# A fused attention and MLP kernel: its instruction order planned anew, with another rule for GpSimd and VectorE at their shared port

## The chip, the cores and the metric

The kernel runs on one core of one Trainium2 chip. What counts is the device time of one execution, in microseconds. Three runs of the kernel before took 1088.69, 1086.15 and 1087.42 us, a median of 1087.42 us. One more execution was profiled; all rows below are from that one.

## What is computed

A linear attention over 8 batches, 8 heads, 576 positions and 64 dimensions, with 128 features and their exponentials of both signs, and behind it an MLP over the 4608 tokens, from 512 to 2048 and back, with the exact GELU:

```python
proj = einsum('bhsd,df->bhsf', x, w_phi)            # x is q, then k
proj = proj - max(abs(proj), axis=-1)
phi = concatenate([exp(proj), exp(-proj)], axis=-1)
kv, z = einsum('bhsf,bhsd->bhfd', k_p, v), k_p.sum(axis=2)
attn = einsum('bhsf,bhfd->bhsd', q_p, kv) / (einsum('bhsf,bhf->bhs', q_p, z) + 1e-6)
x = attn, heads side by side, 4608 x 512
h = x @ w_in                                        # 512 x 2048
out = gelu(h) @ w_out                               # 2048 x 512
```

Both weights arrive as 64-bit floats. The MLP is multiplied in parts: each operand is split into a rounded high part and a low part, and three of the four products are summed.

## The kernel before

**Attention, batch by batch.** For keys, TensorE projects a quarter of a batch's heads into `pk`, VectorE takes the largest absolute value of each row (`mx`, L439) and subtracts it (`ek`, L375), both reading PSUM; ScalarE takes the exponentials, and TensorE sums `kv`. For queries the features lie on the partitions: TensorE makes `pq`, ScalarE copies it to `pc` in SBUF, GpSimd finds the largest of all partitions (`mb`, an all-reduce, L511), VectorE subtracts it, ScalarE takes the exponentials `ef`. From batch 2 on the denominators go another way: VectorE weights the exponentials (two operations of L553 and two of L556, `pc` again), GpSimd adds over the partitions (`db`, L522), and the sums travel through DRAM (`d_d`, `dc`, then `r_d` with the reciprocals of L621). `mb` and `db` have one buffer each.

**Weights.** In `split_weight` each of 32 pieces of 128x512 is turned from two 32-bit words into a float and split: a DMA, an Abs on ScalarE, two operations of VectorE with a scalar (L391, L393), two with a scalar and a tensor (L395, L397), a cast on ScalarE (the high half) and a subtraction on VectorE (L375, the low half). `w_i3_3` is the last piece of the first matrix, `w_o12` to `w_o15` the last four of the second.

**MLP, 18 blocks of 256 tokens.** For block j, `tokens` loads `xr` and the spread reciprocals `xh` (DMAs of L667 and L670), and VectorE makes the product `xr`, its rounded copy `xh` and the rest `xl`. Then eight steps u: 24 matmuls into `ph_j_u`, two GELUs on ScalarE (`gh`, and `ph` in place), the subtraction `gl` on VectorE, and for each of two pieces f the 6 matmuls of `po` that take `gh`, `gl` and `w_o`f. `ph` has two buffers, `po` one. Blocks 0 to 7 run beside the attention of later batches; blocks 8 to 17 use sums of weights (`ts`, L749, made on VectorE beside blocks 2 to 7) to save matmuls, and no attention stands beside them.

**What sets the order.** All operations go into a `Plan`. Its `order` simulates the five engines with a cost for each operation and picks, again and again, the operation that could start first (among those that could start at the same time on one engine, the one with the lowest rank). `emit` then writes the operations by their planned start, and each engine executes its own in that order. The planner has a rule for a port that GpSimd and VectorE share: while a GpSimd all-reduce reads (for `READS` us from its start, `port[1:]`), VectorE's operations with `port` set are not begun. The operations `mx`, `ek` and `gl`, which read PSUM, are exempt (`port=False`). Constants at the file's end set times, biases and slacks.

Of the kernel before, what the change touches and what calls it, by code (L numbers as in the profile page):

```python
# [62 lines left out]
class Plan:  # L63
# [8 lines left out]
    SHAPE = {"f": 0, "k": 1, "q": 1, "v": 2, "n": 2, "w": 3, "d": 4}  # L72
    READS = {"max": 1.12, "add": 2.38, "max main": 1.99, "add main": 4.23, "max rest": 1.0, "add rest": 2.12}
    SPENT = {"max": 2.28, "add": 3.8, "max main": 3.75, "add main": 6.45, "max rest": 2.07, "add rest": 3.42}
    WINDOW = 3.413
# [37 lines left out]
    def order(self, bias):  # L113
# [6 lines left out]
        clock = dict.fromkeys(engines, 0.0)  # L120
# [9 lines left out]
        port = [0.0, 0.0, 0.0]  # L130

        def start_of(o):
            t = max(clock[o.eng], o.ready)
            if o.eng == "pool" and o.port:
                t = max(t, port[0])
            if o.table == "exp" and table[0] == "gelu" and gelus[0] % (2 * STICK):
                t = max(t, left_at[0] + PATIENCE)
            seen = {}
            for b in o.bufs:
                if not b.held and b.tag is not None:  # L140
# [6 lines left out]
                    t = max(t, when)  # L147
                    seen[b.tag] = i + 1
            if o.eng == "dve" and o.port and port[1] <= t < port[2]:
                t = port[2]  # L150
# [21 lines left out]
        while len(done) < n:  # L172
            best = None
            for e, lst in cand.items():
# [3 lines left out]
                for o in lst:  # L178
                    t = start_of(o)
# [12 lines left out]
                key = None  # L192
                for t, o in opts:
                    if t <= lim:
# [5 lines left out]
                        if key is None or (k, o.n) < key[0]:  # L200
                            key = ((k, o.n), t, o)
                if best is None or key[1] < best[1]:
                    best = key
            if best is None:
                raise RuntimeError("no operation can go")
            _, t, o = best
            cand[o.eng].remove(o)
            cost = o.cost
# [3 lines left out]
            if o.eng == "pe":  # L212
                if self.SHAPE[last[0]] != self.SHAPE[o.kind]:
                    cost += self.BEHIND[last[0]] + self.BEFORE[o.kind]
                last[0] = o.kind
            o.start, o.end = t, run(t, cost, o.duty) if o.eng == "pe" else t + cost
            if o.nbytes:
# [3 lines left out]
            if o.table == "gelu":  # L221
                gelus[0] += 1
                left_at[0] = o.end
            clock[o.eng] = o.end + (0.45 if o.eng == "pool" else 0.0)
            if o.eng == "dve" and o.port:
                port[0] = o.end
            if o.eng == "pool" and o.port:
                port[1:] = [o.start, o.start + self.READS[o.port]]
            for b in o.bufs:
# [62 lines left out]
def fused_kernel(ctx: ExitStack, tc: tile.TileContext, qT, kT, va, w_st, w_in, w_out, out):  # L292
# [207 lines left out]
    def q_front(nm, n, load, kb, k, main):  # L500
# [9 lines left out]
        most = f"max{main}"  # L510
        op("pool", plan.SPENT[most], lambda: nc.gpsimd.partition_all_reduce(  # L511
            mb(), pc(), P, bass_isa.ReduceOp.absmax), r=[pc], w=[mb], port=most, **k(1))
# [350 lines left out]
SUMSAT = 177.8  # L863
SUMSEACH = 5.81
SUMSPAN = 311.59
T15 = 926.21
T18 = 982.3
BIAS = 89.44
STICK = 2
# [14 lines left out]
LEAD = 161.66  # L884
HOLD = 13.76
WR = -32.15
ATR = -58.86
AT = 194.75
POOLSLACK = 0.3
DMASLACK = 0.5  # L890
T0 = 91.27
# [43 lines left out]
```

## Time and profile before

| | before |
|---|---|
| median of 3 runs | 1087.42 us |
| the profiled execution, own time | 1086.7 us |
| its span, first to last instruction | 1084.9 us |
| TensorE busy | 1038.2 us (96%) |
| VectorE busy | 697.5 us (64%) |
| ScalarE busy | 616.5 us (57%) |
| GpSimd busy | 305.4 us (28%) |
| mean granted TensorE clock | 0.982 |

In the rows, PE is TensorE, DVE is VectorE, ACT is ScalarE, POOL is GpSimd and SP the engine that issues most DMAs. L12 is line 12 of the kernel. A name as `w_i` stands for all tiles with a number behind it. In a timeline the bracket at a row's end gives the engine's idle time just before it, and what ended it. The clock of a stretch is a share of full speed: 1.00 is 2.4 GHz, 0.50 is 1.2 GHz.

### The profile page before, as it was taken

To read this page: it belongs to the slowest core of one execution; us is meant where nothing else is said; L and a number is where in the kernel's file an instruction comes from. 1 tells how busy PE (TensorE), PEld (TensorE's weight loads), DVE (VectorE), ACT (ScalarE), POOL (GpSimd) and SP (SyncE) were. 2 spreads that over 40 slices of the span, in tenths; PEclk is the share of its full clock that TensorE was granted. 3 is DMA by queue.
4 is the path that set the end of the run, shared out by engine and by line. 5 is a ranking of instruction groups with operands and counts; after the bars stand their busy time and mean duration, and the time that the engine had idled before them with its cause. 6 is when DMAs were issued, how large, how long until landed. Compare 5 with 4: busy or idle time off the path is not lost.

```text
span 1084.9 us, 23613 instructions
## 1 busy us (share of the span) xinstructions
PE 1038.2 (96%) x9763; PEld 900.0 (83%) x9763; DVE 697.5 (64%) x1228; ACT 616.5 (57%) x1008; POOL 305.4 (28%) x77
## 2 busy tenths in 40 slices
PE   7979995999998999999999999999999999999997
PEld 5646664787786787777788879999999999999997
DVE  5999999688977788665344332555565565565554
ACT  4868785666666687667656653434344344344343
POOL 2232234346556453564654451000000000000000
PEclk7999998999999999999999999999999999999999
DMA  8486660344444335324212145620120120120000
GB/s 285 137 249 190 175 218 27 96 134 134 131 128 130 112 127 146 103 66 124 58 55 75 35 126 173 214 59 20 40 60 11 50 60 16 45 59 20 21 21 21
DMA packets 87180, 107.08 MB, mean 99 GB/s; under 512 B 29168, under 2 KB 56832, under 8 KB 87072
## 3 DMA queue, kind: packets, MB, share of 16 engines
q1 hardware_dynamic: 86928, 105.30, 31.9%
q8 instruction: 77, 1.26, 0.5%
q14 instruction: 31, 0.25, 0.1%
q10 hardware_dynamic: 144, 0.26, 0.1%
HBM read 75.87 MB, written 29.66 MB: 97 GB/s over the span
## 4 chain that ended last, share of the span: by engine, by line
PE 80%; DVE 8%; DMA 4%; ACT 3%; issue 3%; POOL 1%; SPq 0%; DVEq 0%; ACTq 0%; POOLq 0%
PE ph L334 33%; PE po L334 14%; PE pa L334 10%; PE pb L334 7%; PE kv L334 5%; PE pn L334 4%; PE pk L334 2%; PE pq L334 2%; DMA xh<-r_d 1%; DMA x_d<-xo 1%; DVE pc L375 1%; DVE pc L553 1%; DVE ts L375 1%; PE pn_rest L334 1%; POOL mb L511 1%
## 5 line engine op out<-in xcount | busy, mean ns | idle before, releaser
L334 PE MATMUL ph<-xh,w_i 128*128 128x256 f32 x2304 | 419.8, 279 | 7.0 <-DVE w_i L375 5.1
L334 PEld LDWEIGHTS ph<-xh,w_i 128*128 128x128 f32 x2304 | 359.4, 189 | 21.0 <-issue 12.2
L334 PE MATMUL ph<-xl,w_i 128*128 128x256 f32 x1152 | 320.1, 278 | 0.0
L334 PEld LDWEIGHTS ph<-xl,w_i 128*128 128x128 f32 x1152 | 217.9, 189 | 0.3
L522 POOL PARTITION_ALL_REDUCE db<-pc x24 | 151.0, 6290 | 137.2 <-DVE pc L556 112.7
L375 DVE TENSOR_TENSOR sg<-ga 128x256 f32<-128x256 f32 (+1 forms) x240 | 84.6, 376 | 153.2 <-ACT ga L780 151.4
L334 PE MATMUL po<-w_o,gh 128*128 128x512 f32 (+1 forms) x518 | 165.8, 402 | 5.0 <-DVE w_o L375 5.0
L511 POOL PARTITION_ALL_REDUCE mb<-pc x36 | 121.2, 3368 | 161.9 <-ACT pc L369 128.2
L780 ACT ACTIVATE ga<-ph 128x512 f32<-128x512 f32 x80 | 47.8, 598 | 168.7 <-PE ph L334 168.7
L334 PEld LDWEIGHTS po<-w_o,gh 128*128 128x128 f32 x518 | 94.5, 190 | 34.4 <-DVE w_o L375 5.3
L334 PE MATMUL pa<-w_o,oh 128*128 128x256 f32 x640 | 112.8, 276 | 0.0
L334 PE MATMUL po<-w_o,gl 128*128 128x512 f32 (+1 forms) x281 | 102.9, 381 | 7.1 <-DVE gl L375 7.1
L334 PEld LDWEIGHTS pa<-w_o,oh 128*128 128x128 f32 x640 | 96.3, 188 | 0.0
L334 PE MATMUL pa<-w_o,ol 128*128 128x256 f32 x320 | 88.3, 276 | 0.0
L375 DVE TENSOR_TENSOR gl<-ph,gh 128x512 fp32r<-128x512 f32 x64 | 43.7, 685 | 67.5 <-ACT ph L704 67.5
L334 PE MATMUL pn<-ef,kvn 128*64 128x512 f32 (+2 forms) x288 | 80.5, 561 | 5.6 <-ACT xo L369 5.6
L334 PE MATMUL pb<-tw,uh 128*128 128x256 f32 x480 | 85.6, 276 | 0.0
L516 ACT ACTIVATE ef<-pc 128x1024 f32<-128x1024 f32 (+1 forms) x72 | 68.1, 972 | 17.5 <-DVE pc L375 17.2
L444 ACT ACTIVATE ek<-ek 128x1024 f32<-128x1024 f32 x64 | 67.6, 1058 | 15.5 <-DVE ek L375 15.0
L334 PEld LDWEIGHTS pb<-tw,uh 128*128 128x128 f32 x480 | 72.2, 188 | 0.0
L334 PEld LDWEIGHTS po<-w_o,gl 128*128 128x128 f32 x281 | 53.9, 192 | 21.3 <-DVE gl L375 9.6
L703 ACT ACTIVATE gh<-ph 128x512 fp32r<-128x512 f32 x64 | 38.2, 597 | 54.2 <-PE ph L334 52.1
(84 smaller groups left out, 1620.8 us busy)
## 6 DMA issues: line engine op xcount, KB each, us to landing
vt<-in_va_dram SPq DMA_DIRECT2D x32, 325.0 KB
t_d<-ts SPq DMA_DIRECT2D x40, 256.0 KB
out_dram<-ob SPq DMA_DIRECT2D x35, 256.0 KB
kt<-in_kT_dram SPq DMA_DIRECT2D x32, 256.0 KB
raw_i<-in_w_in_dram SPq DMA_DIRECT2D x16, 512.0 KB
raw_o<-in_w_out_dram SPq DMA_DIRECT2D x16, 512.0 KB
qt<-in_qT_dram SPq DMA_DIRECT2D x28, 256.0 KB
x_d<-xo SPq DMA_DIRECT2D x24, 256.0 KB
```

Of the source, the lines that this page charges most:

```text
L334: return tc.keep_in_program_order(nc.tensor.matmul(*a, **kw))
L375: op(eng, cost, lambda: e.tensor_tensor(out=dst(), in0=a(), in1=b(), op=o), r=r, w=w, **kw)
L444: op("act", act(256 * n), lambda s=s: nc.scalar.activation(e[s](), e[1](), AF.Exp, scale=1.0 - 2.0 * s), r=[e[1]], w=[e[s]], table="exp", ...
L511: op("pool", plan.SPENT[most], lambda: nc.gpsimd.partition_all_reduce(mb(), pc(), P, bass_isa.ReduceOp.absmax), r=[pc], w=[mb], port=most, ...
L516: op("act", act(2 * n), lambda s=s: nc.scalar.activation(ef[s](), pc(), AF.Exp, scale=1.0 - 2.0 * s), r=[pc], w=[ef[s]], table="exp", **k())
L522: op("pool", plan.SPENT[total], lambda: nc.gpsimd.partition_all_reduce(db(), pc()[:, :2], P, bass_isa.ReduceOp.add), r=[pc], w=[db], port= ...
L553: op("dve", dve(n, fast=True) + 0.06, lambda pc=pc, ef=ef, one=one, j=j: nc.vector.tensor_scalar(out=pc()[:, j], in0=ef[0]()[:, j], scalar ...
L703: op("act", act(2 * TB, True) + 0.016, lambda gh=gh, ph=ph: nc.scalar.activation(gh(), ph(), AF.Gelu), r=[ph], w=[gh], table="gelu", rank= ...
L780: op("act", act(2 * TB, True) + 0.037, lambda ph=ph, ga=ga: nc.scalar.activation(ga(), ph(), AF.Gelu), r=[ph_all], w=[ga], table="gelu", a ...
```

## The change

No operation is added or taken out. The planner is told other things, and the order comes out anew.

- An all-reduce of GpSimd no longer waits in the plan for VectorE's current operation at the port: its place in the order is the time at which its operand is ready. Its work begins when VectorE's operation ends, and from then on VectorE's port operations are held for `READS`.
- Where a GpSimd operation could start at the same time as another engine's, it is put first.
- `READS` grows by 0.07 to 0.22 us an operation, `SPENT` (its whole length) falls by 0.13 to 0.34, and a gap of 0.45 behind each GpSimd operation goes.
- The constants `SUMSEACH` (pace of the weights' sums), `BIAS` (against switching ScalarE's table), `HOLD` (earliest start of batch 1) and `DMASLACK` change.

```diff
@@ Plan
-    READS = {"max": 1.12, "add": 2.38, "max main": 1.99, "add main": 4.23, "max rest": 1.0, "add rest": 2.12}
-    SPENT = {"max": 2.28, "add": 3.8, "max main": 3.75, "add main": 6.45, "max rest": 2.07, "add rest": 3.42}
+    READS = {"max": 1.2, "add": 2.45, "max main": 2.15, "add main": 4.45, "max rest": 1.1, "add rest": 2.2}
+    SPENT = {"max": 2.14, "add": 3.59, "max main": 3.54, "add main": 6.11, "max rest": 1.94, "add rest": 3.23}
@@ start_of
-            if o.eng == "pool" and o.port:
-                t = max(t, port[0])
@@ order
-                if best is None or key[1] < best[1]:
+                if best is None or key[1] < best[1] or key[1] == best[1] and e == "pool":
                     best = key
...
-            o.start, o.end = t, run(t, cost, o.duty) if o.eng == "pe" else t + cost
+            o.start = t
+            if o.eng == "pool" and o.port:
+                t = max(t, port[0])
+                port[1:] = [t, t + self.READS[o.port]]
+            o.end = run(t, cost, o.duty) if o.eng == "pe" else t + cost
...
-            clock[o.eng] = o.end + (0.45 if o.eng == "pool" else 0.0)
+            clock[o.eng] = o.end
...
-            if o.eng == "pool" and o.port:
-                port[1:] = [o.start, o.start + self.READS[o.port]]
@@ constants
-SUMSEACH = 5.81
+SUMSEACH = 5.49
-BIAS = 89.44
+BIAS = 103.27
-HOLD = 13.76
+HOLD = 16.53
-DMASLACK = 0.5
+DMASLACK = 0.3
```

The orders of both kernels hold the same instructions on TensorE, VectorE, GpSimd and SyncE; ScalarE has two loads of its function table fewer. Three places follow, all on VectorE.

**First place: ahead of the low half of `w_i3_3`**, for which the last matmuls of `ph_0_7` wait. The last operation (L556) of `pc_2_0_0` is the operand of the all-reduce `db_2_0_0`. Before:

```order
L556 SCALAR_TENSOR_TENSOR pc_2_0_0_1686<-ef_2_0_0_1_1834,kvn_2_0_0_1376,pc_2_0_0_1686 128x512
L395 SCALAR_TENSOR_TENSOR wt_i3_3_1928<-raw_i3_3_1709,wt_i3_3_1928 128x512
L391 TENSOR_SCALAR wt_o12_1946<-wt_o12_1946 128x512
L397 SCALAR_TENSOR_TENSOR wt_i3_3_1928<-raw_i3_3_1709,wt_i3_3_1928 128x512
L393 TENSOR_SCALAR wt_o12_1946<-wt_o12_1946 128x512
L553 TENSOR_SCALAR pc_2_1_0_1729<-ef_2_1_0_0_1843,kvn_2_0_1_1649 128x512
L395 SCALAR_TENSOR_TENSOR wt_o12_1946<-raw_o12_1774,wt_o12_1946 128x512
L375 TENSOR_TENSOR w_i3_3_1959<-wt_i3_3_1928,w_i3_3_1959 128x512
```

After:

```order
L556 SCALAR_TENSOR_TENSOR pc_2_0_0_1720<-ef_2_0_0_1_1855,kvn_2_0_0_1582,pc_2_0_0_1720 128x512
L397 SCALAR_TENSOR_TENSOR wt_i3_3_1838<-raw_i3_3_1658,wt_i3_3_1838 128x512
L391 TENSOR_SCALAR wt_o12_1885<-wt_o12_1885 128x512
L556 SCALAR_TENSOR_TENSOR pc_2_0_0_1720<-ef_2_0_0_1_1855,kvn_2_0_0_1582,pc_2_0_0_1720 128x512
L375 TENSOR_TENSOR w_i3_3_1937<-wt_i3_3_1838,w_i3_3_1937 128x512
L439 TENSOR_REDUCE mx_2_1_1_1948<-pk_2_1_1_1872 128x8
L375 TENSOR_TENSOR ek_2_1_1_1_1965<-pk_2_1_1_1872,mx_2_1_1_1948 128x1024
L393 TENSOR_SCALAR wt_o12_1885<-wt_o12_1885 128x512
L391 TENSOR_SCALAR wt_o13_1950<-wt_o13_1950 128x512
L395 SCALAR_TENSOR_TENSOR wt_o12_1885<-raw_o12_1717,wt_o12_1885 128x512
```

Five operations (three of `pc_2_1_0`, namely its subtraction and the two of L553, and two of `wt_o12`; some stand above the rows shown) are no longer ahead of `w_i3_3`'s subtraction, and this comes directly behind the operation on which `db_2_0_0` waits.

**Second place: ahead of `w_o15`**, which the matmuls of `po_0` for f = 15 take. The operand of the all-reduce `db_2_1_0` is `pc_2_1_0`; before, its last operation stands 12 rows ahead of the first row here, in front of `w_o13`. Before:

```order
L397 SCALAR_TENSOR_TENSOR wt_o14_1986<-raw_o14_1870,wt_o14_1986 128x512
L391 TENSOR_SCALAR wt_o15_2084<-wt_o15_2084 128x512
L393 TENSOR_SCALAR wt_o15_2084<-wt_o15_2084 128x512
L395 SCALAR_TENSOR_TENSOR wt_o15_2084<-raw_o15_1949,wt_o15_2084 128x512
L375 TENSOR_TENSOR w_o14_2100<-wt_o14_1986,w_o14_2100 128x512
L397 SCALAR_TENSOR_TENSOR wt_o15_2084<-raw_o15_1949,wt_o15_2084 128x512
L375 TENSOR_TENSOR gl_1_0_2145<-ph_1_0_2070,gh_1_0_2126 128x512
L375 TENSOR_TENSOR w_o15_2143<-wt_o15_2084,w_o15_2143 128x512
```

After:

```order
L395 SCALAR_TENSOR_TENSOR wt_o15_2140<-raw_o15_1933,wt_o15_2140 128x512
L375 TENSOR_TENSOR w_o14_2147<-wt_o14_2091,w_o14_2147 128x512
L397 SCALAR_TENSOR_TENSOR wt_o15_2140<-raw_o15_1933,wt_o15_2140 128x512
L556 SCALAR_TENSOR_TENSOR pc_2_1_0_1752<-ef_2_1_0_1_2094,kvn_2_0_1_1848,pc_2_1_0_1752 128x512
L375 TENSOR_TENSOR xr_2_1511<-xr_2_1511,xh_2_2020 128x1024
L375 TENSOR_TENSOR w_o15_2172<-wt_o15_2140,w_o15_2172 128x512
L556 SCALAR_TENSOR_TENSOR pc_2_1_0_1752<-ef_2_1_0_1_2094,kvn_2_0_1_1848,pc_2_1_0_1752 128x512
L371 CAST xh_2_2020<-xr_2_1511 128x1024
L375 TENSOR_TENSOR gl_1_0_2211<-ph_1_0_2030,gh_1_0_2184 128x512
L375 TENSOR_TENSOR er_3_1_2213<-pk_3_r_2013,mx_3_r_2083 128x512
L375 TENSOR_TENSOR gl_1_1_2233<-ph_1_1_2064,gh_1_1_2228 128x512
```

The last operation of `pc_2_1_0` now stands behind `w_o15`, and behind it come one rounding copy, then `gl_1_0`, `er_3_1` and `gl_1_1`, which read PSUM; `gl_1_0` has moved behind `w_o15`, and `xr_2` ahead of it.

**Third place: ahead of `gl_3_0`**, which the first `po` matmuls of block 3 take. Before:

```order
L556 SCALAR_TENSOR_TENSOR pc_4_0_0_3777<-ef_4_0_0_1_3883,kvn_4_0_0_3399,pc_4_0_0_3777 128x512
L375 TENSOR_TENSOR ts_4_4_3910<-ts_4_4_3910 128x256
L556 SCALAR_TENSOR_TENSOR pc_4_0_0_3777<-ef_4_0_0_1_3883,kvn_4_0_0_3399,pc_4_0_0_3777 128x512
L375 TENSOR_TENSOR pc_4_1_0_3832<-pc_4_1_0_3832,mb_4_1_0_3870 128x1024
L375 TENSOR_TENSOR xr_4_3001<-xr_4_3001,xh_4_3745 128x1024
L375 TENSOR_TENSOR gl_3_0_3957<-ph_3_0_3885,gh_3_0_3940 128x512
```

After:

```order
L375 TENSOR_TENSOR gl_2_7_3888<-ph_2_7_3688,gh_2_7_3861 128x512
L375 TENSOR_TENSOR ts_4_4_3826<-ts_4_4_3826 128x256
L375 TENSOR_TENSOR pc_4_0_0_3801<-pc_4_0_0_3801,mb_4_0_0_3842 128x1024
L375 TENSOR_TENSOR gl_3_0_3907<-ph_3_0_3846,gh_3_0_3890 128x512
L439 TENSOR_REDUCE mx_5_0_0_3931<-pk_5_0_0_3911 128x8
L375 TENSOR_TENSOR ts_5_0_3933<-w_o13_2081,w_o5_1154 128x512
L620 TENSOR_SCALAR dc_3_1_3885<-dc_3_1_3885 128x4
L375 TENSOR_TENSOR ek_5_0_0_1_3950<-pk_5_0_0_3911,mx_5_0_0_3931 128x1024
```

Before, `gl_3_0` comes behind `xr_4`, whose operand `xh_4` is loaded by DMAs; after, `xr_4` stands behind `gl_3_1`, and the two last operations of `pc_4_0_0`'s sum behind `gl_3_0` as well. On SyncE the last loads of `xh_4` now stand behind a store of `ts_4_4` and a load of `kt_5_0_1`.

Two more shifts are used below without a listing. On VectorE the `xl_0` of the first block is instruction 94 before and 103 after, with `w_o4`'s and `w_o5`'s first operations, `w_i3_1` and `pc_1_1_0` now ahead of it. On TensorE, all 24 matmuls of `ph_1_0` and 12 of `ph_1_1` now stand ahead of the `po_0` matmuls with `w_o12`, and the attention's `kv_2_1_1` and `pn_2_1_0` ahead of those with `w_o13`; before, `ph_1_0` came in halves behind `w_o12`'s and `w_o13`'s.

## Rows read from the trace of the kernel before

**Rows 1.** The page: busy time of TensorE, and its clock in 40 slices.
```profile
PE 1038.2 (96%) x9763; PEld 900.0 (83%) x9763; DVE 697.5 (64%) x1228; ACT 616.5 (57%) x1008; POOL 305.4 (28%) x77
...
PEclk7999998999999999999999999999999999999999
```

**Rows 2.** Busy time by stretch: stretch, length, each engine's busy time, granted clock, DMA.
```profile
60.00:100.00 40.00, 34.36 (x390) 22.79 (x387) 37.51 (x49) 30.94 (x49) 15.55 (x5) 0.96 0.75 202
...
160.00:200.00 40.00, 26.58 (x221) 23.37 (x220) 34.01 (x41) 19.31 (x28) 13.96 (x2) 0.83 0.17 55
200.00:340.00 140.00, 138.48 (x1472) 111.23 (x1471) 114.69 (x155) 96.76 (x146) 76.39 (x18) 1.00 0.43 133
...
360.00:660.00 300.00, 298.36 (x2795) 239.68 (x2794) 164.78 (x221) 199.91 (x269) 162.75 (x37) 1.00 0.32 93
660.00:1079.00 419.00, 419.00 (x3662) 417.51 (x3661) 225.27 (x585) 167.24 (x365) 0.00 (x0) 1.00 0.17 54
```

**Rows 3.** Timeline of TensorE, 158 to 363 us: start, length, operation, idle before.
```profile
163.33 0.39 PE L334 MATMUL ph<-xh,w_i 128*128 128x256 f32 x1 [1.97 <-ACT w_i L369]
...
168.89 0.79 PE L334 MATMUL ph<-xh,w_i 128*128 128x256 f32 x2 [5.06 <-DVE w_i L375]
...
176.43 0.71 PE L334 MATMUL pk_r<-wst,kr 64*128 64x128 f32 x8 [1.34 <-DVE ek L375]
...
188.10 0.79 PE L334 MATMUL po<-w_o,gh 128*128 128x512 f32 x1 [5.04 <-DVE w_o L375]
...
351.22 0.79 PE L334 MATMUL po<-w_o,gl 128*128 128x512 f32 x1 [4.38 <-DVE gl L375]
```

**Rows 4.** Busy time in three stretches of the lower clock (columns as rows 2).
```profile
165.60:172.30 6.70, 3.41 (x16) 3.41 (x17) 6.70 (x10) 1.91 (x3) 3.33 (x1) 0.50 0.00 0
...
186.10:192.80 6.70, 4.70 (x18) 4.31 (x18) 4.94 (x7) 0.62 (x1) 0.34 (x1) 0.50 0.00 0
349.90:356.60 6.70, 5.38 (x16) 4.51 (x17) 6.67 (x10) 2.34 (x2) 1.17 (x1) 0.50 0.11 40
```

**Rows 5.** Timeline of VectorE, 155 to 200 us.
```profile
158.67 0.48 DVE L553 TENSOR_SCALAR pc<-ef,kvn 128x512 f32<-128x512 f32 x1
...
162.88 4.76 DVE L553 TENSOR_SCALAR pc<-ef,kvn 128x512 f32<-128x512 f32 x1
...
168.16 0.68 DVE L375 TENSOR_TENSOR w_i<-wt_i,w_i 128x512 fp32r<-128x512 f32 x1
...
180.59 4.56 DVE L391 TENSOR_SCALAR wt_o<-wt_o 128x512 f32<-128x512 f32 x1
185.18 1.54 DVE L393 TENSOR_SCALAR wt_o<-wt_o 128x512 uint32<-128x512 uint32 x1
...
189.39 0.69 DVE L375 TENSOR_TENSOR w_o<-wt_o,w_o 128x512 fp32r<-128x512 f32 x1
```

**Rows 6.** Timeline of GpSimd: one mb and the three db of these places.
```profile
146.90 3.54 POOL L511 PARTITION_ALL_REDUCE mb<-pc  x1 [3.25 <-DVE pc L375]
...
161.17 7.76 POOL L522 PARTITION_ALL_REDUCE db<-pc  x1 [10.73 <-DVE pc L556]
180.24 6.20 POOL L522 PARTITION_ALL_REDUCE db<-pc  x1 [11.31 <-DMA d_d<-db]
...
344.05 7.02 POOL L522 PARTITION_ALL_REDUCE db<-pc  x1 [3.09 <-DVE pc L556]
```

**Rows 7.** Timeline of VectorE beside the mb at 146.90 us.
```profile
147.25 1.21 DVE L439 TENSOR_REDUCE mx<-pk 128x8 f32<-128x1024 f32 x1
148.50 1.23 DVE L375 TENSOR_TENSOR ek<-pk,mx 128x1024 f32<-128x1024 f32 x1
```

**Rows 8.** Timeline of VectorE, 338 to 361 us.
```profile
346.60 3.97 DVE L375 TENSOR_TENSOR xr<-xr,xh 128x1024 f32<-128x1024 f32 x1 [1.51 <-DMA xh<-r_d]
350.49 0.68 DVE L375 TENSOR_TENSOR gl<-ph,gh 128x512 fp32r<-128x512 f32 x1
```

**Rows 9.** Busy time from 330 to 410 us (columns as rows 2).
```profile
330.00:410.00 80.00, 75.62 (x786) 60.47 (x785) 63.46 (x84) 58.56 (x83) 41.44 (x9) 0.96 0.40 124
```

**Rows 10.** Timeline of TensorE, 60 to 100 us.
```profile
78.87 1.19 PE L334 MATMUL pn<-ef,kvn 128*65 128x288 f32 x4 [3.19 <-ACT xo L369]
```

## The prediction, made before the change was timed

> **What bounds the kernel now.** The page's totals come first: TensorE is busy 1038.2 us [rows 1] of a span of 1084.9, so all other engines together cost it 46.7 us. The clock's 40 slices show where: it is low at the start, in the slice from 163 on, and nowhere else by much [rows 1]. The table by stretch says it sharper. From 160 to 200 TensorE works 26.58 of 40 us at a clock of 0.83; from 200 to 340 it loses 1.5 us, from 360 to 660 1.6, and behind that nothing [rows 2]. So whatever TensorE loses before 360 us arrives at the end one for one, since nothing later has slack to give it back, and what stops it before 200 and at 350 is what an order can change. The timeline of TensorE names those stops: 1.97, 5.06, 1.34 and 5.04 us between 160 and 190, all for weights or for VectorE's `ek`, and 4.38 us at 351 for `gl` [rows 3]. Behind each long stop the clock stands at 0.50, that is 1.2 GHz, for a stretch [rows 4]: TensorE had stood idle just before, and pays for the stop twice.
>
> Why VectorE is late there is read from its own timeline. An operation with a scalar that takes 0.48 us at 158.67 takes 4.76 at 162.88, and two more take 4.56 and 1.54 at 180.59 and 185.18 [rows 5]. Beside them GpSimd's two `db` all-reduces run, from 161.17 and from 180.24 [rows 6]. Operations that read PSUM are not held: `mx` and `ek` keep 1.21 and 1.23 us beside the `mb` at 146.90 [rows 6, 7]. So a hold costs the path only if what stands behind it on VectorE is awaited by TensorE, and behind these two stand the low halves of `w_i3_3` and of `w_o15` [rows 5].
>
> **The change, part by part.** It moves work, adds none, and the sum is therefore made of stops that go and stops that come. It is made against the profiled execution, 1086.7 us, which lies 0.7 under the median of the runs shown.
>
> *First and second place.* The four stops there come to 1.97 + 5.06 + 1.34 + 5.04 = 13.4 us. In the two slow stretches TensorE does 3.41 and 4.70 us of work [rows 4], which at the full clock takes half: (3.41 + 4.70) / 2 = 4.1 us more. Together 17.5 us could go.
>
> How much does? `w_i3_3` is ready at 168.16 + 0.68 = 168.84. In the new order five operations are no longer ahead of it, 2 x 0.48 + 0.42 + 0.68 + 1.23 = 3.3 us (the 0.42 from operations of the same form in that timeline, the 0.68 and the 1.23 from [rows 5, 7]), and the hold, 4.76 - 0.48 = 4.3 us, falls behind it: 168.8 - 3.3 - 4.3 = 161.2, when TensorE has just got there. That stop goes, and the ScalarE half of it with it, since its operand comes earlier by the same operations. The hold does not vanish. It now meets `wt_o12`, first covered by `mx` and `ek` of batch 2 (2.4 us, reading PSUM), and it still delays `gl_0_6`, which stands four operations behind: I put it at 168.1. As `ph` has two buffers, `ph_1_0` waits for that: some 1.5 us of a stop remain. The second hold, 4.08 and some 1.1 us, fell ahead of `w_o15`; now its operand is ready only behind `w_o15`, one operation of 0.68 may still meet it, and then `gl_1_0`, `er_3_1` and `gl_1_1` pass. Counting VectorE's operations through, `w_o15` comes at 181.8 + 1.1 = 182.9 instead of 189.39 + 0.69 = 190.1; TensorE, not stopped before, wants it about 1.5 us earlier. On GpSimd nothing else is queued behind these two `db`s until 202 that a batch needs sooner.
>
> One thing speaks against this. `xl_0` now has nine more operations ahead, some 5.6 us at these durations, so the first MLP block may begin later by 0 to 5.6 us. VectorE is busy 37.51 of 40 us there [rows 2], so little of it is hidden by idleness; but attention operations that TensorE would have done in between now come earlier, and holds in the old order fall away. I take 2.0. First and second place: 17.5 - 1.5 - 1.5 - 2.0 = 12.5 us, between 9 (the whole 5.6 lost) and 15.
>
> *Third place.* `xr_4` is held until 350.57 and `gl_3_0` behind it until 351.2 [rows 8], while `db_4_0_0` runs [rows 6]. In the new order `gl_3_0` stands ahead of `xr_4` and of the operations on which that `db` waits. The 4.38 us go, and half of the 5.38 us of work in the slow stretch behind it [rows 4]: 4.4 + 2.7 = 7.1 us. What is late next is `xl_4`, wanted only by block 4, some 60 us on.
>
> *What comes.* TensorE's order has one change of kind more, which my count of its rows prices at 0.5 us (0 to 1). And an earlier TensorE asks for `gl` earlier: from 330 to 410 VectorE is busy 63.46 of 80 us with the stop in it [rows 9], and none of that work becomes less. I allow for one new stop of the size of the one at 351, 4.4 us (0 to 7.1, the whole of the third place). What it would be exactly, the trace of before can't show, as TensorE is late there already.
>
> Sum: -12.5 - 7.1 + 0.5 + 4.4 = -14.7, so 1086.7 - 14.7 = 1072.0 us.
>
> A rule to be weighed. The rows show a `db` that began at 161.17 and ended at 168.93, while the held operation had ended at 167.64, and VectorE's other operations ran for 1.7 us beside its start [rows 5, 6]. The Trainium skill, "SBUF — State Buffer", section "Who interferes with whom", says that whoever issues first gets the shared ports "for the whole instruction" and the other fully blocks. By that, a hold would last to the end of `db`, 1.3 us longer here, and `gl_0_6` would come 1.3 us later, so 1073.3. The row decides for the shorter hold at the first place; at the second the two slow operations together end at 186.72 where `db` ends at 186.44, so there the rule nearly fits.
>
> **The rivals.** *Only the first half comes.* If VectorE is what sets the pace from 330 to 410, the 7.1 us of the third place return as stops at later `gl`s. For it speaks that it is 79% busy there and that a `db` hold is 4.3 us each time; against it, that from 360 to 660 TensorE loses 1.6 us in 300. Time: 1086.7 - 12.5 + 0.5 + 4.4 = 1079.1, from 1077 to 1084 with the first places at their lower end and a second stop.
>
> *It doesn't do what it says.* GpSimd's operations begin at the same events as before; only a plan is different. If the holds fall on operations as urgent as before (on `gl_0_6` for a full 4.3, on a `w_o` for another), the first places keep only the 3.3 us of removed work less the 2.0 of a late start, and a stop like the third one comes back: about 1086, no change.
>
> *Slower.* The mechanism is the start: from 60 to 100 TensorE already waits 3.19 us for ScalarE's `xo` [rows 10], and VectorE is at 94%. In the new order `pk_1_1_0`, two weights and `xr_0` (whose `xh_0` comes by DMA) stand where VectorE must wait for another engine. Were each of those four and `ph_0_0` itself a stop of 3.19, 16 us, with the 5.6 of `xl_0`'s shift in full, TensorE would reach 160 us 21.6 later instead of 2.0: 1072.0 + 19.6 = 1091.6, and around 1089 to 1094. It decides from 14.7 us of loss at the start beyond my 2.0. Against it: VectorE has idle time of 2.5 us in that stretch, not of sixteen, and the stops could run into one another.
>
> **How the numbers follow.** The forecast (both gains, at most one new stop, 1066 to 1077) has 0.55; the first rival 0.20; no change 0.07; slower 0.11; better than 1066, if no new stop comes and the start isn't late (17.5 - 3 + 7.1 = 21.6, 1065), 0.07. The range takes the forecast, the first rival and the upper part of the better case: 1065 to 1084. A measurement of this kernel can tell about 0.2%, or 2.2 us, from no change. Faster by more than that: 0.55 + 0.20 + 0.07 = 0.82; within it 0.07; slower 0.11.
>
> **What the new profile would show.** If the first place is right, no stop of TensorE over 2 us stands between 160 and 190, the clock of that stretch is near 1.00, and `po_0` for `w_o15` ends some 12 us earlier; the `db` holds still appear, on `wt_o` and behind `w_o15`. If the third is right, `gl_3_0` runs ahead of the held `xr_4`. Stops on `gl` between 330 and 410 of over 5 us, or an `xl_0` more than 4 us late, would make me wrong in the ways above; so would a slow stretch of the clock at a place that has none now.

## The result, and the profile after

The changed kernel took 1067.51, 1075.56, 1072.99 and 1072.62 us, a median of 1072.8, against 1087.76 for four runs of the kernel before: a ratio of 0.986 with a 95% interval of 0.982 to 0.990, some 15 us less (between 11 and 20). A later comparison, five runs beside fifteen of before, had 1068.15 against 1087.25, a ratio of 0.983 (0.980 to 0.986). The ratio takes fourteen of the fifteen; the one left out took 2061.50 us, and why is not known. The nine executions of the changed kernel fall into two groups, four from 1066.8 to 1068.2 and five from 1072.6 to 1075.6; the others of the kernel before lie between 1085.0 and 1090.1. The execution profiled first is the one of 1067.51, with a span of 1065.7, which is 19.2 us under the profiled execution of before. All rows of "after" are from it. Below, a stop is idle time of TensorE, and a hold is a VectorE operation that takes several times its usual length beside an all-reduce of GpSimd.

The page of after, first the busy time, then the clock by slices:

```profile
PE 1033.3 (97%) x9765; PEld 897.1 (84%) x9765; DVE 683.6 (64%) x1228; ACT 615.4 (58%) x1006; POOL 306.4 (29%) x77
...
PEclk7999999999999999999999999999999999999999
```

TensorE does the same work (1033.3 us, before 1038.2 [rows 1]; the mean granted clock is 0.991 instead of 0.982) and is idle 32.4 us of the span instead of 46.7. The low slice at 163 us has gone. By stretch (length; busy time of TensorE, its weight loads, VectorE, ScalarE, GpSimd; clock; DMA share; GB/s):

```profile
60.00:100.00 40.00, 32.83 (x372) 20.07 (x372) 35.32 (x50) 30.39 (x49) 16.47 (x5) 1.00 0.79 221
...
160.00:200.00 40.00, 37.34 (x306) 30.99 (x308) 33.86 (x49) 28.21 (x41) 19.77 (x4) 0.96 0.34 108
200.00:340.00 140.00, 138.83 (x1494) 111.56 (x1493) 116.77 (x161) 99.31 (x146) 75.07 (x17) 1.00 0.43 131
340.00:360.00 20.00, 20.00 (x237) 15.11 (x236) 15.87 (x20) 13.00 (x20) 12.27 (x3) 1.00 0.43 129
360.00:660.00 300.00, 299.30 (x2704) 246.15 (x2702) 156.48 (x213) 191.08 (x255) 154.75 (x35) 1.00 0.34 96
```

From 160 to 200 TensorE works 37.34 us where it worked 26.58 [rows 2], at 0.96 instead of 0.83, and from 340 to 360 it has no idle time. The stops that are left in the timeline of TensorE from 100 to 200 (start, length, operation, idle before):

```profile
100.55 1.93 PE L334 MATMUL pn<-ef,kvn 128*65 128x512 f32 x4 [1.50 <-ACT xo L369]
153.58 1.08 PE L334 MATMUL pn<-ef,kvn 128*64 128x512 f32 x4 [0.52 <-ACT ef L516]
159.96 0.50 PE L334 MATMUL ph<-xh,w_i 128*128 128x256 f32 x2 [0.28 <-DVE w_i L375]
167.74 0.39 PE L334 MATMUL ph<-xh,w_i 128*128 128x256 f32 x1 [2.66 <-DVE gl L375]
```

The stop of 5.06 us for `w_i3_3` in [rows 3] is down to 0.28 (in both kernels TensorE stands at `ph_0_6` there, not at `ph_0_7`), and the one of 5.04 us is gone. That one was not for `w_o15`, as the prediction has it. It ended at 188.10, when the low half of `w_o14` was ready (187.37 + 0.68 = 188.05), which stood behind the same hold; `w_o15` was ready at 190.08, and TensorE took it at 195.50 without a stop. VectorE before:

```profile
187.37 0.68 DVE L375 TENSOR_TENSOR w_o<-wt_o,w_o 128x512 fp32r<-128x512 f32 x1
```

What remains in after is 2.66 us for `gl_0_6`. VectorE's timeline shows where the holds went, and GpSimd's below it the all-reduces that make them:

```profile
159.23 0.68 DVE L375 TENSOR_TENSOR w_i<-wt_i,w_i 128x512 fp32r<-128x512 f32 x1
159.83 1.21 DVE L439 TENSOR_REDUCE mx<-pk 128x8 f32<-128x1024 f32 x1
161.14 1.23 DVE L375 TENSOR_TENSOR ek<-pk,mx 128x1024 f32<-128x1024 f32 x1
162.28 2.30 DVE L393 TENSOR_SCALAR wt_o<-wt_o 128x512 uint32<-128x512 uint32 x1
164.50 1.65 DVE L391 TENSOR_SCALAR wt_o<-wt_o 128x512 f32<-128x512 f32 x1
...
167.01 0.68 DVE L375 TENSOR_TENSOR gl<-ph,gh 128x512 fp32r<-128x512 f32 x1
...
180.54 0.69 DVE L375 TENSOR_TENSOR w_o<-wt_o,w_o 128x512 fp32r<-128x512 f32 x1 [0.39 <-ACT w_o L369]
```
```profile
159.39 6.48 POOL L522 PARTITION_ALL_REDUCE db<-pc  x1 [4.96 <-DVE pc L556]
182.05 6.42 POOL L522 PARTITION_ALL_REDUCE db<-pc  x1 [16.18 <-DVE pc L556]
```

`w_i3_3` is ready at 159.91 instead of 168.84: `db_2_0_0` begins only 0.16 us after its subtraction, which keeps its length. Beside this all-reduce, the reduction and the subtraction that read PSUM keep theirs too, and 3.1 us of hold are left for two operations of `wt_o` (2.30 and 1.65 instead of 0.41 each). `gl_0_6` is late for two reasons: ScalarE's GELU, behind a table load of 1.28 us, ends at 165.86, and VectorE takes it at 167.01, behind the held operations. `w_o14` is now ready at 177.75 instead of 188.05, and `w_o15` at 181.23 instead of 190.08. The second all-reduce begins behind both and holds almost nothing: the copy `xh_2` keeps 0.69 us, `gl_1_0`, `er_3_1` and `gl_1_1` read PSUM, and `xl_2` takes 1.38 us at 186.59 instead of 1.22. In the kernel before it began late, at 180.24, not for its operand (ready at 172.04) but for the DMA that empties `db`'s one buffer [rows 6]. The third place, VectorE's timeline from 325 to 342 us:

```profile
325.30 0.69 DVE L375 TENSOR_TENSOR gl<-ph,gh 128x512 fp32r<-128x512 f32 x1
...
334.70 0.69 DVE L375 TENSOR_TENSOR gl<-ph,gh 128x512 fp32r<-128x512 f32 x1 [0.41 <-ACT ph L704]
...
339.08 3.04 DVE L375 TENSOR_TENSOR xr<-xr,xh 128x1024 f32<-128x1024 f32 x1
```

`gl_3_0` (325.30) runs long before `db_4_0_0` begins at 336.14, and `gl_3_1` (334.70) too. `xr_4` is held behind them (3.04 us for 1.22), and TensorE does not stop for it.

### The profile page after: what moved, and what is told of

Same layout as the page of the kernel before. It is cut to its first block, busy times and chain, and to the rows that moved or that the text cites. A ratio compares the mean times of both kernels' runs of the same rounds, so it can differ in the third digit from the quotient of the medians.

```text
span 1065.7 us, 23642 instructions
## 1 busy us (share of the span) xinstructions
PE 1033.3 (97%) x9765; PEld 897.1 (84%) x9765; DVE 683.6 (64%) x1228; ACT 615.4 (58%) x1006; POOL 306.4 (29%) x77
## 4 chain that ended last, share of the span: by engine, by line
PE 83%; DVE 9%; DMA 3%; ACT 3%; issue 2%; SPq 1%; POOL 0%; DVEq 0%; ACTq 0%
PE ph L334 33%; PE po L334 16%; PE pa L334 10%; PE pb L334 7%; PE kv L334 6%; PE pn L334 5%; PE pk L334 3%; PE pq L334 2%; DMA xh<-r_d 1%; DVE mx L439 1%; PE pn_rest L334 1%; DVE ek L375 1%; DVE pc L375 1%; DVE w_i L375 1%; DVE ts L375 1%
## 5 line engine op out<-in xcount | busy, mean ns | idle before, releaser
L334 PEld LDWEIGHTS ph<-xh,w_i 128*128 128x128 f32 x2304 | 357.6, 189 | 12.9 <-issue 7.6
L369 ACT CAST uh<-sg 128x384 fp32r<-128x384 f32 x80 | 41.3, 516 | 46.5 <-DVE sg L375 46.5
L334 PE MATMUL kv<-vt,ek 128*64 128x65 f32 x2048 | 66.5, 224 | 0.7 <-ACT ek L444 0.7
```

Source lines behind the costliest of these rows:

```text
L334: return tc.keep_in_program_order(nc.tensor.matmul(*a, **kw))
L369: op(eng, cost, lambda: nc.scalar.copy(out=dst(), in_=src()), r=r, w=w, **kw)
```

## The experiments

All were built so that the plan stays as it is and single operations are moved in the finished order (`MOVES`, a list of "this operation, behind that one"; the helper that reads it is not shown), unless the text says otherwise. Long lines are shown in part, and cuts are marked with dots. Each run is given with its ratio to runs of the kernel before on the same chip, and gains are against their median.

### Are the holds the cause? Three of them nearly taken away

```diff
- ... nc.gpsimd.partition_all_reduce(db(), pc()[:, :2], P, bass_isa.ReduceOp.add) ...
+ ... nc.gpsimd.partition_all_reduce(db()[:, :, :32] if nm in SHORT else db(),
+ ...  pc()[:, :2, :32] if nm in SHORT else pc()[:, :2], P, bass_isa.ReduceOp.add) ...
...
- ... in_=db()[:1] ...
+ ... in_=pc()[:1] if nm in SHORT else db()[:1] ...
+ SHORT = ('2_0_0', '2_1_0', '4_0_0')
```

> The kernel before, in its own order; three of GpSimd's 24 db all-reduces (db_2_0_0, db_2_1_0, db_4_0_0) are made over 32 of 512 columns, and the DMA that carries their sums away takes the first row of pc instead, so that the denominators of these three pieces are other numbers. Theory (the holds are what makes the three places late): the 4.3 us of hold ahead of w_i3_3, the 5.2 ahead of w_o15 and the 2.7 ahead of gl_3_0 go; TensorE's stops of 5.06 and 5.04 us shrink to under 1.5, the one of 4.38 to about 1.6, and with half of the slow stretches 12 to 17 us go: 1070 to 1075. Rival (VectorE has simply too much to do there, and the holds are hidden by other waits): not under 1083.

Measured: 1071.98 us (1070.58 to 1073.28), a ratio of 0.986 (0.984 to 0.987). The order is that of before, instruction for instruction; the three all-reduces take 2.35, 2.28 and 1.62 us instead of 7.76, 6.20 and 7.02. As the DMA reads `pc`, the second no longer waits for one either and begins at 168.79 instead of 180.24, so at this place the hold went by its length and by its time together. TensorE's stops, in the same places as [rows 3]:

```profile
164.19 0.39 PE L334 MATMUL ph<-xh,w_i 128*128 128x256 f32 x1 [1.97 <-ACT w_i L369]
165.48 0.51 PE L334 MATMUL ph<-xh,w_i 128*128 128x256 f32 x2 [0.78 <-DVE w_i L375]
173.02 0.71 PE L334 MATMUL pk_r<-wst,kr 64*128 64x128 f32 x8 [1.41 <-DVE ek L375]
...
337.85 0.50 PE L334 MATMUL po<-w_o,gl 128*128 128x512 f32 x1 [1.77 <-DVE gl L375]
```

The stop of 5.06 is 0.78, that of 5.04 is gone, that of 4.38 is 1.77. So three holds, without any new order, were worth as much as the whole change. That is what the theory says, and the time lies in its range.

### The third place alone

```diff
+ MOVES = [(('dve', 'xr_4', -1), ('dve', 'gl_3_0', -1))]
```

> The kernel before with one pair exchanged on VectorE: gl_3_0 stands ahead of xr_4. Theory: the stop of 4.38 us and half of the 5.38 us of work in the slow stretch behind it go, 7.1 us in all, and nothing takes their place: 1079 to 1081. Rival (xl_4 or a later gl is late instead, since VectorE sets the pace from 330 to 410): under 3 us gained, over 1083.5.

Measured: 1083.52 (1082.65 to 1084.4), 0.9963 (0.9949 to 0.9977), so a gain of 3.7 us, where the theory had 7.1 and the rival under 3; the time lies at the rival's edge. But what was late was neither `xl_4` nor a later `gl`. VectorE and then TensorE of this kernel:

```profile
345.08 0.68 DVE L375 TENSOR_TENSOR gl<-ph,gh 128x512 fp32r<-128x512 f32 x1
346.25 4.39 DVE L375 TENSOR_TENSOR xr<-xr,xh 128x1024 f32<-128x1024 f32 x1 [0.48 <-DMA xh<-r_d]
350.56 1.21 DVE L439 TENSOR_REDUCE mx<-pk 128x8 f32<-128x1024 f32 x1
351.81 1.22 DVE L375 TENSOR_TENSOR ek<-pk,mx 128x1024 f32<-128x1024 f32 x1
```
```profile
358.94 2.52 PE L334 MATMUL kv<-vt,ek 128*64 128x65 f32 x60 [1.98 <-ACT ek L444]
```

`gl_3_0` is in time, and the next operation behind the held `xr_4` that TensorE waits for is `ek_5_0_0`: a new stop of 1.98 us, and a stretch around it (358 to 363) at a clock of 0.71. A second version has `xr_4` behind that one too:

```diff
+ MOVES = [(('dve', 'xr_4', -1), ('dve', 'ek_5_0_0_1', 0))]
```

> The kernel before with xr_4 on VectorE behind gl_3_0 and also behind mx_5_0_0 and ek_5_0_0, where b_gl_first had it behind gl_3_0 alone. Theory (b_gl_first gave 3.7 of the 7.1 us that the prediction had for the third place, because ek_5_0_0 still stood behind the held xr_4 and stopped TensorE at kv_5_0_0 for 1.98 us, with a stretch at a clock of 0.71 behind it): that stop goes and some 3 us more come, 6 to 7.5 in all: 1079 to 1081. Rival (the rest of the third place's price was never there): 1082.5 to 1084, as b_gl_first.

Measured: 1080.46 (1079.65 to 1081.14), 0.9936 (0.9922 to 0.9949): 7.2 us, and no stop of TensorE from 330 to 365. The prediction's price of the third place, 7.1, was right, but it is the price of two exchanges, not of one.

### The first two places alone

```diff
+ MOVES = [(('dve', 'pc_2_0_0', -1), ('dve', 'w_i3_3', -1)), (('dve', 'pc_2_1_0', -1), ('dve', 'w_o15', -1))]
```

> The kernel before with two VectorE operations moved: the last operation of pc_2_0_0 (operand of db_2_0_0) stands behind w_i3_3's subtraction, the last of pc_2_1_0 (operand of db_2_1_0) behind w_o15's. Theory: the stop of 5.06 us on w_i3_3 goes nearly whole, since its hold (4.3) and 0.7 of work fall behind it; the first hold still stands ahead of w_o12, so some 2 to 3 us of stop come there; w_o15 comes 5.9 us earlier (second hold and 0.7). Sum 5 to 9 us: 1078 to 1082. Rival (it needs the whole new order, as only that takes work off VectorE ahead of w_i3_3): at most 2 us gained, over 1084.

Measured: 1088.31 (1086.16 to 1089.58), 1.0006 (0.9996 to 1.0017). It was no test of what it was made for: the all-reduce `db_2_1_0` was left where it stood in the program, so it takes its sums before the last term of `pc_2_1_0` is added, and holds VectorE ahead of `w_o14` and `w_o15` as before (4.76 and 1.54 us at 182.78 and 187.57). With the all-reduces and the second one's DMA moved along:

```diff
+ MOVES = [(('dve', 'pc_2_0_0', -1), ('dve', 'w_i3_3', -1)), (('pool', 'db_2_0_0', -1), ('dve', 'pc_2_0_0', -1)),
+          (('dve', 'pc_2_1_0', -1), ('dve', 'w_o15', -1)), (('pool', 'db_2_1_0', -1), ('dve', 'pc_2_1_0', -1)),
+          (('sp', 'of db_2_1_0', -1), ('pool', 'db_2_1_0', -1))]
```

> The kernel before with the all-reduces db_2_0_0 and db_2_1_0 and the last VectorE operation of their operands (and the second's DMA) moved behind the low halves of w_i3_3 and of w_o15. Theory: the stop of 5.06 us on w_i3_3 goes nearly whole, the one of 5.04 on w_o15 too; the first hold falls on w_o12, where 2 to 3 us of stop come: 1078 to 1082. Rival (two moves aren't enough, since VectorE is behind with all its work there): over 1084.

Measured: 1083.65 (1081.51 to 1084.73), 0.9971 (0.9959 to 0.9984), a gain of 3.0 us where 5 to 9 were expected. TensorE's stops:

```profile
165.08 0.39 PE L334 MATMUL ph<-xh,w_i 128*128 128x256 f32 x1 [1.41 <-ACT w_i L369]
166.37 0.50 PE L334 MATMUL ph<-xh,w_i 128*128 128x256 f32 x2 [0.78 <-DVE w_i L375]
179.28 1.23 PE L334 MATMUL pk_r<-wst,kr 64*128 64x128 f32 x8 [6.82 <-DVE ek L375]
```

Both named stops went as expected (5.06 to 0.78, and 5.04 to nothing). But the first hold, now behind `w_i3_3`, still stood ahead of `ek_2_1_1`, as in the kernel before. TensorE, no longer stopped by `w_i3_3`, came there earlier and waited 6.82 us instead of 1.34. I had expected it on `w_o12`, with 2 to 3. In the changed kernel `mx` and `ek` stand directly behind `w_i3_3`, inside the hold. So a hold moved from one awaited operation to another gained 3.0 us here; to gain more it has to meet operations that nobody awaits, or those that read PSUM.

### Putting one hold back into the changed kernel

```diff
+ MOVES = [(('dve', 'w_o15', -1), ('dve', 'xh_2', -1))]
```

> The changed kernel with one operation moved: the low half of w_o15 stands behind the copy xh_2, and so behind the operation that lets db_2_1_0 begin, as it did in the kernel before. Theory: it is held until some 4.6 to 6.4 us after that all-reduce begins (181 to 182), gl_1_0 behind it too; TensorE stops for 3 to 5 us at po_0 for w_o15, and half of the slow stretch behind it comes on top: 4.5 to 7.5 us more than the changed kernel's 1068 to 1073. Rival (TensorE finds other work, or w_o15 slips ahead of the hold as the copy did): the same as the changed kernel within 1 us.

Measured: 1069.14 (1067.02 to 1076.89), 0.985 (0.981 to 0.989), the same as the changed kernel: the rival was right. VectorE, then GpSimd, in this kernel:

```profile
184.14 0.69 DVE L371 CAST xh<-xr 128x1024 fp32r<-128x1024 f32 x1
184.74 0.69 DVE L375 TENSOR_TENSOR w_o<-wt_o,w_o 128x512 fp32r<-128x512 f32 x1
186.13 0.69 DVE L375 TENSOR_TENSOR gl<-ph,gh 128x512 fp32r<-128x512 f32 x1 [0.70 <-ACT ph L704]
...
189.79 1.22 DVE L375 TENSOR_TENSOR xl<-xr,xh 128x1024 fp32r<-128x1024 f32 x1
```
```profile
184.38 7.02 POOL L522 PARTITION_ALL_REDUCE db<-pc  x1 [15.09 <-DVE pc L556]
```

`w_o15` begins 0.36 us after the all-reduce and takes its usual 0.69. VectorE came with no gap from one operation to the next, and the all-reduce was longer (7.02 us, in after 6.42). It is therefore not enough to say that an operation stands behind the operand of an all-reduce; which one is held is decided a little later. The run can't tell what a held `w_o15` would cost, as the hold did not come back.

### Why the changed kernel has two groups of times

> The changed kernel as it is, for its spread: its profiled execution took 1067.5 us and three others 1072.6 to 1075.6. Theory: median 1072 to 1074, and the slower executions have one stop of 3 to 5 us more at a place where TensorE's margin is small (330 to 410 us, as the prediction's allowance has it). Rival: the difference sits in the first 100 us, in DMA and hand-offs, and delays all that follows.

Measured: 1074.02, 1066.83, 1068.15, 1074.66 and 1067.63 us, a median of 1068.15, under the 1072 to 1074 expected. The profile was of the first, 1074.02, and so a member of the slower group can be laid beside after. TensorE in it:

```profile
82.82 3.68 PE L334 MATMUL pn<-ef,kvn 128*65 128x512 f32 x4 [3.46 <-ACT ef L516]
...
607.23 0.80 PE L334 MATMUL po<-w_o,gl 128*128 128x512 f32 x1 [2.94 <-DVE gl L375]
```

After has 1.61 us at the first and no stop at the second. Behind the second, the stretch from 607 to 614 has a clock of 0.76. VectorE at the two places, in this execution:

```profile
79.32 1.23 DVE L375 TENSOR_TENSOR xr<-xr,xh 128x1024 f32<-128x1024 f32 x1 [1.75 <-DMA xh<-r_d]
...
601.37 5.20 DVE L375 TENSOR_TENSOR xr<-xr,xh 128x1024 f32<-128x1024 f32 x1 [0.57 <-DMA xh<-r_d]
606.50 0.68 DVE L375 TENSOR_TENSOR gl<-ph,gh 128x512 fp32r<-128x512 f32 x1
```

and in after, 598.52 being the same operation as 601.37:

```profile
77.07 1.22 DVE L375 TENSOR_TENSOR xr<-xr,xh 128x1024 f32<-128x1024 f32 x1
...
598.52 1.23 DVE L375 TENSOR_TENSOR xr<-xr,xh 128x1024 f32<-128x1024 f32 x1
599.66 0.69 DVE L375 TENSOR_TENSOR gl<-ph,gh 128x512 fp32r<-128x512 f32 x1
```

At 77 us a DMA of `xh_0` comes late, and VectorE stands still for 1.75 us with `pc_1_0_0` queued behind, whose exponentials TensorE awaits. At 600 us `xr_8` waits 0.57 us for its `xh_8`. In that time the all-reduce `db_7_1_0` begins (600.96), `xr_8` is held for 4 us, and `gl_7_0` with it: the pattern of the third place, at another block. In after `xr_8` follows without a gap and begins 0.23 us ahead of the all-reduce. Whether the DMA or the all-reduce comes first is thus a race. So one part of the difference lies in the first 100 us, as the rival has it, and the other in one stop, but at 607 us and not between 330 and 410. A kernel with `xr_8` and `xr_0` behind the awaited operations:

```diff
+ MOVES = [(('dve', 'xr_8', 0), ('dve', 'gl_7_0', -1)), (('dve', 'xr_0', 0), ('dve', 'ek_1_1_1_1', 0))]
```

> The changed kernel with two pairs exchanged on VectorE: xr_8 behind gl_7_0 (at 600 us), and xr_0 behind pc_1_0_0, mx_1_1_1 and ek_1_1_1 (at 77 us). Theory (an execution of the changed kernel is slow when a DMA of xh comes late: xr_0 then holds up VectorE by 1.75 us at 79, and xr_8 starts behind db_7_1_0, is held for 4 us and gl_7_0 behind it stops TensorE for 2.9 us at 607): both stops no longer depend on these DMAs; all executions between 1064 and 1069, median 1066 to 1067. Rival (the two stops are only where a delay from elsewhere shows): executions still spread from 1067 to 1075.

Measured: 1066.43 us, executions of 1066.32, 1067.22, 1066.55 and 1066.09; a ratio of 0.982 (0.980 to 0.983). The spread of 9 us has become one of 1.1. The same two moves stand in the two kernels of the next section, whose four executions each spread by 0.9 and 1.8 us, so none of twelve was of a slower group. That both places are the cause of the slower group is so shown for the two together; each by itself was not run. For their shares there are two hints. The profiled execution of a_w15_late, of 1070.45 us, has the first alone: VectorE waits 2.23 us for `xh_0` there, TensorE stops for 3.93 us at 82.50, no stop stands near 600, and the time is 2.9 us over after. And in a_xr a stop of 2.69 us is left at 81.28, as ScalarE's copy `xo` there waits 2.40 us for another DMA (of `x_d`). So the larger share seems to be that of the second place.

### What is left at 167 us, and a faster version

Two attempts at the 2.66 us on `gl_0_6`. In the first `gl_0_7` came to stand ahead of the second GELU of `ph_0_7`, so that it subtracts from the values before it (the two moves of `a_xr` stand in both kernels beside what is shown):

```diff
+ MOVES = [(('dve', 'wt_o12', 1), ('dve', 'gl_0_6', -1)), (('dve', 'wt_o12', 2), ('dve', 'wt_o12', 1)), (('dve', 'wt_o12', 3), ('dve', 'wt_o12', 2)),
+          (('dve', 'wt_o13', 0), ('dve', 'wt_o12', 3)), (('dve', 'gl_0_7', -1), ('dve', 'wt_o13', 0)), (('dve', 'wt_o13', 1), ('dve', 'gl_0_7', -1)),
+          (('dve', 'wt_o13', 2), ('dve', 'wt_o13', 1)), (('act', 'ek_2_1_1_0', 0), ('act', 'ph_0_7', -1))]
```

> As a_xr, and beside it at 162 to 170 us: ScalarE does the GELUs of ph_0_6 and ph_0_7 ahead of the exponentials of ek_2_1_1, and VectorE's gl_0_6 and gl_0_7 stand ahead of operations of wt_o12 and wt_o13 that db_2_0_0 holds. Theory (the 2.66 us stop of TensorE at 167.7 is gl_0_6 behind a hold and behind a table load, and the 4 us at a clock of 0.65 behind it follow from it): 2.7 and 1.4 us go, less up to 1.5 for w_o12, which is then wanted earlier: 1062 to 1064.5. Rival (w_o12 and w_o13 are late instead): 1066 to 1068, as a_xr.

Measured: 1066.32 (1065.87 to 1066.72), 0.9815 (0.980 to 0.983), as a_xr; the stop at 167 had gone, and one of 2.22 us for ScalarE's high half of `w_o12` at 171 had come, as the rival says. What it gained at one stop it lost at the other. The second has this high half ahead of the exponentials, and `gl_0_7` where it was:

```diff
+ MOVES = [(('dve', 'wt_o12', 1), ('dve', 'gl_0_6', -1)), (('dve', 'wt_o12', 2), ('dve', 'wt_o12', 1)), (('dve', 'wt_o12', 3), ('dve', 'wt_o12', 2)),
+          (('dve', 'wt_o13', 0), ('dve', 'gl_0_7', -1)), (('dve', 'wt_o13', 1), ('dve', 'wt_o13', 0)),
+          (('act', 'w_o12', -1), ('act', 'ph_0_7', -1)), (('act', 'ek_2_1_1_0', 0), ('act', 'w_o12', -1))]
```

> The changed kernel with xr_0 and xr_8 behind their neighbours as in a_xr, and at 162 to 170 us: ScalarE does the GELUs of ph_0_6 and ph_0_7 and the high half of w_o12 ahead of the first exponential of ek_2_1_1; VectorE does gl_0_6 ahead of wt_o12's operations, and these ahead of gl_0_7 and of wt_o13's. Theory: the stop of 2.65 us at 167.6 and the 4 us at a clock of 0.65 behind it (1.4 us) go, and no stop on w_o12 takes their place, since its high half is cast at 166: 1062 to 1063.5. Rival (the stop moves to w_o13 or kv_2_1_1, as one of 2.2 us on w_o12 took its place in a_best): 1065.5 to 1067.

Measured: 1064.14 us (1062.97 to 1064.77), 0.979 (0.978 to 0.981), the fastest of all, though 0.6 us over the range of the theory; its lowest execution lies in that range, and all four under the rival's. In its stretch from 160 to 200 the clock is whole:

```profile
160.00:200.00 40.00, 38.89 (x329) 30.55 (x329) 38.20 (x54) 31.03 (x44) 19.48 (x5) 1.00 0.36 115
```

### Which part of the diff

Two plans with half of the diff each (the constants are put on one line here). First the new rule alone, with the old tables and constants:

```diff
  (against after)
- READS = {"max": 1.2, "add": 2.45, ...
+ READS = {"max": 1.12, "add": 2.38, ...
- SPENT = {"max": 2.14, "add": 3.59, ...
+ SPENT = {"max": 2.28, "add": 3.8, ...
- SUMSEACH, BIAS, HOLD, DMASLACK = 5.49, 103.27, 16.53, 0.3
+ SUMSEACH, BIAS, HOLD, DMASLACK = 5.81, 89.44, 13.76, 0.5
```

> The planner with the new rule alone (an all-reduce placed when its operand is ready, GpSimd first among equals, no gap of 0.45), with the old READS, SPENT and constants. Its order has w_i3_3 and w_o15 ahead of the operands of db_2_0_0 and db_2_1_0, and gl_3_0 ahead of xr_4. Theory (what decides is where the holds fall, whichever number made the order): 1066 to 1076. Rival (the new constants matter of themselves): 1080 or more.

Measured: 1078.61 (1077.07 to 1080.34), 0.993 (0.991 to 0.994), between theory and rival. All three places are in order in it, and none of the stops of [rows 3] over 0.5 us is left. The rest of the gain is lost elsewhere: TensorE is idle 39.7 us, in after 32.4, with these stops among them:

```profile
103.40 0.39 PE L334 MATMUL ph<-xl,w_i 128*128 128x256 f32 x1 [2.95 <-DVE xl L375]
...
160.01 2.08 PE L334 MATMUL pk<-wst,kt 64*128 64x128 f32 x16 [3.38 <-DVE ek L375]
...
298.08 1.40 PE L334 MATMUL pk<-wst,kt 64*128 64x128 f32 x16 [2.73 <-ACT pc L369]
...
357.81 1.16 PE L334 MATMUL pk<-wst,kt 64*128 64x128 f32 x16 [1.89 <-DMA kt<-in_kT_dram]
```

Then everything but the rule:

```diff
  (against before)
- READS = {"max": 1.12, "add": 2.38, ...
+ READS = {"max": 1.2, "add": 2.45, ...
- SPENT = {"max": 2.28, "add": 3.8, ...
+ SPENT = {"max": 2.14, "add": 3.59, ...
- SUMSEACH, BIAS, HOLD, DMASLACK = 5.81, 89.44, 13.76, 0.5
+ SUMSEACH, BIAS, HOLD, DMASLACK = 5.49, 103.27, 16.53, 0.3
```

> The planner with everything but the new rule: the new READS, SPENT and constants, and an all-reduce that waits in the plan for VectorE's operation, with the gap of 0.45. Its order has w_i3_3 ahead of the operand of db_2_0_0, w_o15 directly behind the last operation of db_2_1_0's operand (as w_i3_3 stands in the changed kernel), and gl_3_0 ahead of xr_4. Theory (the place of the holds decides, not which part of the diff put them there): 1066 to 1077. Rival (the rule is what brings the gain): 1083 or more.

Measured: 1074.25 (1073.08 to 1076.47), 0.989 (0.987 to 0.991), as the theory has it: most of the gain comes without the rule. Each half moves operations in the whole program, so these two runs tell that the place of the holds matters more than the reason why the planner put them there. They do not tell what the rule is worth by itself.

## Why the prediction was right, step by step

Forecast 1072.0, measured 1072.8. The mechanism, that holds ahead of awaited operations stop TensorE, is shown by b_short_db, and by b_ek_first for the third place. Its terms did not all have the right size, and one was not what it was taken for. That the median agrees to 0.8 us is luck: it depends on how many executions fall into each of the two groups, and the later five gave 1068.15.

**First and second place, 12.5 us.** Of the 17.5 us of stops and slow clock, 0.28 and 2.66 us of stops are left, and some 1.7 us of slow clock from 169 to 173 (4 us at a mean clock of 0.57). So 12.9 us went. The matmuls with `w_o15` begin 12.0 us earlier, a rough measure, as other matmuls stand ahead of them now. `w_i3_3` came 8.9 us earlier (7.6 were worked out). The remaining stop on `gl_0_6` was 2.66 instead of 1.5, and the prediction had no slow clock behind it. Its 1.5 at `w_o15` did not come: the prediction took the stop of 5.04 us for one on `w_o15`, and it was one on `w_o14`, 2.0 us earlier on VectorE. The hold was the right one, so the price of the stop stood.

**The late start, 2.0 us.** `xl_0` was ready at 90.42 instead of 86.97, so 3.5 us later, near the middle of the bounds of 0 and 5.6. TensorE waited 0.77 us for it, as attention matmuls filled the rest. In sum the start cost nothing that shows: from 60 to 160 TensorE was idle 8.5 us instead of 7.5, and the clock from 60 to 100 was 1.00 instead of 0.96. In the slower execution the start is 2.3 us later still, by the DMA at 77 us, which is the hand-off that the slower rival named (`xr_0`, whose `xh_0` comes by DMA). It came at a tenth of the 21.6 us that this rival needed.

**Third place, 7.1 us.** In after the stop is gone, and b_ek_first measures 7.2 for this place alone. b_gl_first shows what the prediction had passed over: "what is late next" was not `xl_4` but `ek_5_0_0`, which the changed order also puts ahead of `xr_4`.

**The new stop, 4.4 us.** This is the term that was wrong in kind. There is no such stop from 330 to 410, where it was expected because VectorE has so much to do: there TensorE is busy 80.00 of 80 us. In the execution profiled first, behind 168 us, none is longer than 1.23 us (at 663). It lies at 1067.5, near the 1067.6 that the sum gives without this term: 12.9 and 7.1 us of gains come to 20.0, of which 19.2 show between the profiled executions, and the 0.8 between them is not assigned to a place. In the slower execution there is one, of 2.94 us and a stretch at 0.76 (0.24 x 7, some 1.7 us), at 607. Its cause is no load of VectorE but a DMA for which VectorE stands idle 0.57 us. The median of 1072.8 lies at the forecast because three of those four executions, and five of all nine, are of the slower group; one of that group was profiled. So the allowance for one new stop was met by a stop of another cause. Of the signs that the prediction named, one did not come true: a stop of over 2 us is left between 160 and 190, the one of 2.66.

**The rule that was weighed.** The row at the first place was taken for a hold that ends 1.3 us ahead of the all-reduce's end. In after two operations of `wt_o` are slow one behind the other, to 166.15, where the all-reduce ends at 165.87. So the end of the all-reduce was the better measure there, as at the second place of before. The Trainium skill ("SBUF — State Buffer", section "Who interferes with whom") says that whoever issues first gets the shared port pair "for the whole instruction". The traces agree at these two places, but not at others: at the first place of before the hold ended 1.3 us ahead of the all-reduce, and in a_w15_late `xl_2` kept its 1.22 us at 189.79, beside an all-reduce that ended at 191.40. About the beginning they disagree too: `w_o15` in a_w15_late began 0.36 us after the all-reduce and was not held.

**The rivals.** "Only the first half comes" gave 1079.1, in a range from 1077, and no execution of the changed kernel lay there. "It doesn't do what it says" is refuted by the rows of the first place: the holds fell on other operations.

## What to carry to other kernels

Where GpSimd all-reduces run beside VectorE, look in its timeline for operations of several times their usual length, and then for who waits for what stands behind them. Such a hold costs nothing where nobody waits for what stands behind it, so an order that puts the awaited operation, or operations that read PSUM, directly behind the operand of the all-reduce can gain the hold and the slow clock after the stop. Take the name of what TensorE waits for from the moment at which the stop ends: here `w_o14` was ready 0.05 us before it, and `w_o15` 2 us after it. Operations that wait for a DMA do not belong ahead of an awaited one at such a place: a DMA that is half a microsecond late made a hold of 4 us, and moving two such operations took the spread of executions from 9 us to 1.

## What the runs showed of the hardware that was not expected

- The start of a GpSimd all-reduce is not the start of its hold, as far as the profile's rough times of GpSimd tell. Operations that come with no gap on VectorE kept their length beside it, 0.36 us after its start (184.74) and up to 1.4 us after it (162.54 in the kernel before), and these all-reduces took 7.02 and 7.76 us, against 6.11 for most of the others of their kind. Where VectorE paused for 0.57 us, the next operation was held for 4 us.
- An add all-reduce over 64 columns of 128 partitions took 1.62 to 2.35 us (b_short_db), one over 1024 columns 6.11, so the time falls far less than the columns.
- In after, the stop of 2.66 us at 167.74 was followed by a stretch at a mean clock of 0.57 (169 to 173), so mostly at 1.2 GHz. Stops of 2.22 us (a_best) and 1.98 us (b_gl_first) were followed by 0.72 (171 to 177) and 0.64 (359 to 363). In a_best2, without this stop, the clock from 160 to 200 was 1.00, that is 2.4 GHz, though a stop of 0.94 us was still there (170.32).
